# Global scores without repeats, first loads in parts, w_val decoded in pairs, a third buffer for x, a new order

## Chip, core and metric

The kernel runs on one core of one Trainium2 chip. The metric is the time of one execution on the device in microseconds (us). TensorE multiplies matrices, VectorE and ScalarE work on tiles of 128 partitions, and the queues of SyncE (SP) and ScalarE (ACT) start the transfers (DMA). TensorE writes to PSUM, which has eight banks of 512 fp32 columns; all else lies in SBUF.

## What is computed

Attention for 8 batches of 8 heads with 512 local and 32 global positions, head size 64. A global query sees all keys, a local one the global keys and the local keys at most 32 away. The result, as a sequence of 544 positions of 512 values, goes through a causal convolution of 5 taps that makes a gate, and two 512 x 512 matrices:

```python
s_g = scale * np.matmul(q_g, k_all.transpose(0, 1, 3, 2))   # k_all: 32 global keys, then 512 local
out_g = np.matmul(sm(s_g), v_all)
mask = np.abs(pos[:, None] - pos[None, :]) <= 32
s_l = np.concatenate([scale * q_l @ k_g.T, np.where(mask, scale * q_l @ k_l.T, -1e9)], axis=-1)
out_l = np.matmul(sm(s_l), v_all)
x = concatenate([out_g, out_l])        # to (8, 544, 512)
gate = sigmoid(sum(conv_w[k] * xp[:, k:k + S, :] for k in range(5)))
return (gate * (x @ w_val)) @ w_out
```

All inputs and outputs are fp32, but the three arrays of weights lie in memory as 64-bit floats.

## The kernel before

**Units.** Two heads of a batch make one of 32 units; four units make a batch. `qk` is a unit's load: 48 blocks of 32 columns, 16 of local queries, one of global queries, 31 of keys (`KEYS`, L36), in which the block of global keys stands in several places, so that the five blocks that a window of queries needs can be read with one stride (`window`, L59).

**Local attention.** `l_s` (L428) makes the scores of a unit: 32 matmul calls of a 64 x 32 tile each, eight side by side on TensorE. What lies outside the window has to be masked. Where the order names `ngN` for a unit (`ON_PE`, L187; units 0 to 15), TensorE adds the mask by 8 matmuls of 512 columns with the bf16 constants `far` and 4 small ones (L434, L440); VectorE then makes the maximum with two plain reductions over PSUM (`l_max`, L465) and a scaling (`l_neg`, L474), and ScalarE's exponential reads PSUM (L482). In the other units VectorE adds the mask, makes the maximum and writes to SBUF, in eight instructions of 128 columns (L469), and the exponential reads SBUF. Then come the reciprocal, the normalization (`l_norm`, on ScalarE or VectorE), a transpose on VectorE (`l_turn`, L507) and for two units together the product with the values (`l_av`, L513: ten groups, "slots", of eight tiles).

**Global attention.** Once a batch `g_s` (L354) makes the scores of its 32 global queries for all heads: 640 columns for each half of the heads, of which 544 are keys and 96 are repeats that the layout of the values weighs with zero. `g_max` (L370) copies the scores to SBUF and takes the maximum, `g_exp` (L376) makes the exponential from SBUF, `g_t` and `g_tc` transpose and copy (five 128 x 128 blocks for each half, one buffer `pgt`), `g_av` (L395) multiplies with the values, once for each half.

**The rest.** The result of a unit is copied to `xc` (two buffers), split into `xh` and `xl`, and run through the taps: on TensorE for units 0 to 3 (`pc`, with diagonal matrices `dg`), else four steps on VectorE (L567). A sigmoid, the first matrix (`g1`, L606, three matmuls for each product), the gate (`gv`), a split (`gh`, `gl`) and the second matrix (`g2`, L643) follow, then the copy out (`ob`) and the store (`st`). The global rows of all batches go through the same at the very end.

**Weights.** `weight(k)` (L290) loads and decodes the 64-bit floats of `w_val` (0 to 3, a block of columns each) and `w_out` (4 to 7) in eight steps `wK.s0` to `wK.s7` on VectorE (`s0` may be on ScalarE) and one, `wK.high`, on either; a step covers 128 x 512.

**Order.** All tasks stand in one list written out by hand, `ORDER` (L75); every engine takes its own in that order. `:ACT` or `:DVE` names the engine, `@` the PSUM banks. `zN` are N matmuls of zeros. The loads come first, in the order `FIRST` (L180, "q0 q1 w0 q2 q3 w1 v0 w2 w3 v1 m0") on SP's queue; the conv weights and `far` are on ScalarE's (L754, L756). Later loads (`iq`, `ig`, `iv`, `wi`) wait for the matmul ahead of them in the list.

Of the kernel before, what the change touches and what calls it, by code (L numbers as in the profile page):

```python
# [32 lines left out]
GQ = NC  # L33
K0 = GQ + 1
PAIRED = (3, 6, 9, 12, 15)
KEYS = [x for c in range(NC) for x in ((c, -1) if c % 3 == 2 else (c,))] + [x for c in PAIRED for x in (c, -1)]  # L36
NB = K0 + len(KEYS)
AT = {c: K0 + c + c // 3 for c in range(NC)}
WITH_G = {c: K0 + NC + NC // 3 + 2 * n for n, c in enumerate(PAIRED)}

# [3 lines left out]
GC = (R + 1) * R * C  # L44
GB = (R + 1) * R - 1
assert KEYS[AT[NC - 1] - K0:][:R + 1][-1] == -1

# [28 lines left out]
cw dg0:DVE dg1:DVE w0.s0:DVE w0.s1 z6.0@0 s0@64 mx0.0 mx0.1 ng0 dg2:ACT dg3:ACT w0.s2 s1@01 z6.1@2 s2@23 exp0.0 exp0.1  # L76
mx1.0 w0.s3 mx1.1 w0.s4 ng1 exp1.0 w0.s5 w1.s0:DVE w0.s6 w1.s1 den0 w0.s7 mx2.0 rec0 exp1.1 ig2 norm0.0:ACT w1.s2 den1
wi4 w0.high:DVE rec1 norm1.0:ACT norm1.1:ACT norm0.1:DVE gs0@46 mx2.1 w3.s0:ACT gmax0.0 ng2 t0 t1 z20.2@0 av0@40 w3.s1
w1.s3 iq4 exp2.0 exp2.1 gexp0.0 xc0:ACT gmax0.1 w1.s4 w3.s2 den2 w1.high:ACT iq5 w1.s5 rec2 norm2.1:ACT w1.s6 halo0
w1.s7 w3.s3 w4.s0:DVE ig3 ig0 gt0.0@2 w4.s1 pc0.0@6 xh0:ACT xl0 xc1:ACT w4.s2 ig1 s3@45 mx3.0 mx3.1 halo1 w4.s3 ng3  # L80
w4.s4 w3.s4 w4.s5 w3.s5 gtc0.0 pc0.1 pc0.2 pc0.3 pc0.4 norm2.0:ACT w3.high:ACT t2 pc1.0@2 xh1:ACT s4@01 exp3.0 exp3.1
conv0.3:ACT w4.s6 w4.high:ACT den3 mx4.0 rec3 mx4.1 iq6 w4.s7 wi5 w3.s6 ng4 pc1.1 norm3.0:DVE gav0.0@5 gexp0.1 gt0.1@6
w3.s7 norm3.1:ACT t3 pc1.2 s5@43 mx5.0 mx5.1 gtc0.1 iq7 exp4.0 w2.s0:ACT w2.s1 exp4.1 ng5 gav0.1 w5.s0:ACT gden0 pc1.3
w2.s2 grec0 exp5.0 exp5.1 pc1.4 xl1 av1@60 xc2:ACT gnorm0 w5.s1 gx0@4 gxc0:ACT conv1.3:ACT w2.s3 den4 w5.s2 w2.s4 rec4
g1.0.1.0@5 w5.s3 xc3:ACT w2.s5 w5.high:ACT xh2:DVE norm4.0:ACT den5 gs1@63 iq8 halo2:DVE w5.s4 ig4 rec5 xl2 iq9
gmax1.0 w5.s5 s6@21 pc2.0@6 mx6.0 g1.0.1.1 xh3:DVE iv2 mx6.1 w5.s6 ng6 w2.s6 gexp1.0 w5.s7 norm4.1:ACT halo3:DVE s7@70
mx7.0 mx7.1 w2.high:DVE norm5.0:ACT ng7 t4 norm5.1:ACT t5 exp6.0 exp6.1 den6 exp7.0 pc2.1 pc2.2 pc2.3 xl3 fix1 wi6
pc2.4 pc3.0@2 pc3.1 rec6 gmax1.1 norm6.1:DVE pc3.2 fix0 exp7.1 pc3.3 den7 w2.s7 pc3.4 ig5 av2@03 norm6.0:ACT rec7
conv3.3:ACT ig6 conv2.3:ACT t6 w6.s0:ACT sig0 gt1.0@6 w6.s1 wi7 g1.0.0.0@2 g1.0.0.1 xc5:ACT norm7.1:DVE s8@34 ig7 sig1
w6.s2 norm7.0:DVE w6.s3 t7 xc4:ACT s9@10 g1.0.0.2 w6.s4 mx8.0 mx8.1 iq10 g1.0.0.3 sig2 mx9.0 w7.s0:DVE w6.s5 gv.0.0  # L90
g1.0.1.2 g1.0.1.3 iq11 gtc1.0 gav1.0@7 ng8 w7.s1 g1.0.2.0@2 w6.s6 sig3 gv.0.1 w6.high:ACT gexp1.1 gt1.1@5 w6.s7 w7.s2
mx9.1 w7.s3 g1.0.2.1 xh4:ACT gh.0.0:ACT gl.0.0 ng9 exp8.0 g1.0.2.2 exp8.1 den8 iv3 gtc1.1 xl4 exp9.0 w7.s4 gh.0.1:ACT
g1.0.2.3 gv.0.2 exp9.1 gav1.1 gden1 s10@56 rec8 ig9 grec1 gs2@13 w7.s5 iq12 gnorm1 gx1@7 tap4:ACT mx10.0 mx10.1
norm8.0:ACT w7.s6 xh5:ACT den9 gmax2.0 ig10 iq13 gxc1:ACT gl.0.1 w7.high:ACT ig11 ng10 tap5:DVE gexp2.0 halo4:ACT
g1.0.3.0@0 g1.0.3.1 g1.0.3.2 gmax2.1 g1.0.3.3 s11@72 gh.0.2:ACT iv4 gv.0.3 halo5:ACT w7.s7 rec9 conv4.0 gl.0.2 xl5 ig8
# [10 lines left out]
g1.1.3.1 g1.1.1.3 xl8 exp13.0 exp13.1 ng15 g1.1.3.2 g1.1.3.3 gv.1.1 exp15.0 exp15.1 av5@51 conv9.1 ig15 iv7 conv8.0
gh.1.1:ACT conv9.2 g1.1.2.2 g1.1.2.3 conv8.1 conv9.3 conv8.2 xc10:ACT den13 conv8.3 gs3@46 gh.1.0:ACT xc11:ACT iq16
iq17 rec13 norm13.1:ACT iq18 gl.1.0 g2.1.2.0@1 g2.1.1.0@2 gl.1.1 iq19 gv.1.2 den15 xh10:ACT gv.1.3 rec15 gmax3.0
st.0.3:ACT halo10:ACT g2.1.0.0@3 g2.1.2.1 gh.1.2:DVE g2.1.1.1 gh.1.3:DVE gl.1.2 halo11:ACT tap11:ACT norm13.0:ACT
gexp3.0 g2.1.0.1 gl.1.3 g2.1.0.2 gmax3.1 tap10:ACT rec14 t13 gt3.0@4 gtc3.0 xh11:DVE norm14.0:ACT norm14.1:DVE t14  # L110
# [73 lines left out]
NG = 2  # L184
# [8 lines left out]
def attention_moe(ctx, tc, qk, vw, vgw, maskd, fard, w_val, convT, w_out, out):  # L193
# [96 lines left out]
    def weight(k):  # L290
# [30 lines left out]
        for n in range(8):  # L321
            tasks[f"w{k}.s{n}"] = lambda n=n: step(n)
# [517 lines left out]
```

## Time and profile before

| | us |
|---|---|
| median of 3 runs | 353.23 |
| lowest and highest | 350.35, 353.97 |
| the profiled execution | 350.34 |
| its span, first to last instruction | 348.5 |

The profile is of one execution. PE is TensorE's matmuls, PEld its weight loads (which overlap matmuls), DVE VectorE, ACT ScalarE. A matmul's end in the trace is modelled, and neighbouring instructions of one engine overlap in it, so the time from one start to the next says what one really costs. PEclk is the granted share of TensorE's clock.

### The profile page before, as it was taken

To read this page: it belongs to the slowest core of one execution; us is meant where nothing else is said; L and a number is where in the kernel's file an instruction comes from. 1 tells how busy PE (TensorE), PEld (TensorE's weight loads), DVE (VectorE), ACT (ScalarE), POOL (GpSimd) and SP (SyncE) were. 2 spreads that over 40 slices of the span, in tenths; PEclk is the share of its full clock that TensorE was granted. 3 is DMA by queue.
4 is the path that set the end of the run, shared out by engine and by line. 5 is a ranking of instruction groups with operands and counts; after the bars stand their busy time and mean duration, and the time that the engine had idled before them with its cause. 6 is when DMAs were issued, how large, how long until landed. Compare 5 with 4: busy or idle time off the path is not lost.

```text
span 348.5 us, 15657 instructions
## 1 busy us (share of the span) xinstructions
PE 334.3 (96%) x6712; PEld 257.7 (74%) x6712; DVE 318.0 (91%) x863; ACT 282.8 (81%) x930; POOL 1.0 (0%) x8
## 2 busy tenths in 40 slices
PE   7879999999999999999999999999999999999995
PEld 4565665867877777787887878777877888788784
DVE  4899999989999899999999999999999997986961
ACT  3799999998998987998999999999887768144140
POOL 1000000000000000000000000000000000000000
PEclk9999999999999999999999999999999999999998
DMA  8958756679467195752823956536530332001032
GB/s 291 382 216 297 244 163 211 214 233 350 138 226 218 26 392 172 235 192 89 293 91 86 396 206 184 184 103 199 171 137 2 115 112 89 4 30 60 32 120 60
DMA packets 19748, 60.67 MB, mean 174 GB/s; under 512 B 2272, under 2 KB 4704, under 8 KB 19680
## 3 DMA queue, kind: packets, MB, share of 16 engines
q1 hardware_dynamic: 17664, 56.47, 47.4%
q10 hardware_dynamic: 2016, 3.22, 2.6%
q8 instruction: 52, 0.85, 1.0%
q14 instruction: 16, 0.13, 0.1%
HBM read 50.76 MB, written 8.91 MB: 171 GB/s over the span
## 4 chain that ended last, share of the span: by engine, by line
PE 78%; DMA 7%; DVE 6%; ACT 5%; issue 1%; SPq 1%; DVEq 0%; ACTq 0%
PE psum L606 25%; PE psum L643 22%; PE psum L521 10%; PE psum L448 7%; PE psum L584 5%; DMA qk<-in_qk_dram 4%; DMA wraw<-in_w_val_dram 3%; PE psum L401 3%; PE psum L385 3%; PE psum L366 3%; ACT pm L482 2%; ACT pm L498 1%; DVE gateg L681 1%; SPq L283 1%; DVE mx L465 1%
## 5 line engine op out<-in xcount | busy, mean ns | idle before, releaser
L567 DVE SCALAR_TENSOR_TENSOR gate<-xc,cw,gate 128x512 f32<-128x512 f32 x112 | 81.2, 745 | 1.0
L606 PE MATMUL psum<-xh,wvh 128*128 128x512 f32 x128 | 53.2, 416 | 0.5 <-ACT pm L482 0.5
L606 PE MATMUL psum<-xl,wvh 128*128 128x512 f32 x128 | 50.9, 398 | 1.1 <-issue 1.0
L643 PE MATMUL psum<-woh,gh 128*128 128x512 f32 x128 | 51.6, 403 | 0.0
L498 ACT ACTIVATE pm<-pm,mx 128x128 f32<-128x128 f32 x156 | 49.8, 416 | 1.8 <-DVE mx L492 1.8
L482 ACT ACTIVATE pm<-pm,mx 128x128 f32<-128x128 f32 x128 | 49.7, 394 | 1.6 <-DVE mx L469 1.5
L643 PE MATMUL psum<-woh,gl 128*128 128x512 f32 x128 | 50.2, 392 | 0.8 <-DVE gl L620 0.8
L606 PE MATMUL psum<-xh,wvl 128*128 128x512 f32 x128 | 50.4, 394 | 0.0
L643 PE MATMUL psum<-wol,gh 128*128 128x512 f32 x128 | 50.0, 391 | 0.0
L482 ACT ACTIVATE pm<-psum,mx 128x128 f32<-128x128 f32 x128 | 45.1, 405 | 1.4 <-DVE mx L474 1.3
L521 PEld LDWEIGHTS psum<-pts,v 32*64 32x64 f32 x2560 | 35.8, 130 | 9.7 <-DVE pts L507 2.3
L521 PE MATMUL psum<-pts,v 32*64 32x96 f32 (+3 forms) x2560 | 39.5, 258 | 2.0 <-DVE pts L507 1.9
L448 PE MATMUL psum<-qk 64*32 64x128 f32 x2048 | 37.6, 272 | 2.7 <-issue 1.5
L507 DVE STREAM_TRANSPOSE pts<-pm 128x1024 f32<-128x1024 f32 x32 | 39.0, 1229 | 0.6 <-ACT pm L498 0.3
L448 PEld LDWEIGHTS psum<-qk 64*32 64x32 f32 x2048 | 31.6, 105 | 7.6 <-issue 3.8
L482 ACT ACTIVATION_READ_ACCUMULATOR pm<-psum,mx 128x1 f32 x128 | 31.5, 246 | 0.0
L606 PEld LDWEIGHTS psum<-xh,wvh 128*128 128x128 f32 x128 | 24.5, 191 | 7.1 <-issue 1.2
L643 PEld LDWEIGHTS psum<-woh,gl 128*128 128x128 f32 x128 | 24.0, 188 | 6.6 <-DVE gl L620 1.2
L469 DVE CUSTOM_DVE_ANT_0 pm<-psum,mask 128x128 f32<-128x128 f32 x128 | 28.4, 284 | 0.4 <-PE psum L448 0.3
L606 PEld LDWEIGHTS psum<-xh,wvl 128*128 128x128 f32 x128 | 24.0, 188 | 6.0 <-issue 0.6
L606 PEld LDWEIGHTS psum<-xl,wvh 128*128 128x128 f32 x128 | 24.1, 188 | 5.8 <-issue 1.7
L643 PEld LDWEIGHTS psum<-woh,gh 128*128 128x128 f32 x128 | 24.1, 188 | 5.6 <-issue 0.7
(122 smaller groups left out, 591.3 us busy)
## 6 DMA issues: line engine op xcount, KB each, us to landing
qk<-in_qk_dram SPq DMA_DIRECT2D x32, 768.0 KB, 6.1
vg<-in_vgw_dram SPq DMA_DIRECT2D x32, 325.0 KB, 4.2
v<-in_vw_dram SPq DMA_DIRECT2D x16, 640.0 KB, 4.9
out_dram<-ob SPq DMA_DIRECT2D x21, 256.0 KB, 3.4
out_dram<-ob ACTq DMA_DIRECT2D x11, 256.0 KB, 3.0
wraw<-in_w_val_dram SPq DMA_DIRECT2D x4, 512.0 KB, 12.1
wraw<-in_w_out_dram SPq DMA_DIRECT2D x4, 512.0 KB, 4.8
out_dram<-obg ACTq DMA_DIRECT2D x1, 256.0 KB, 3.1
```

Of the source, the lines that this page charges most:

```text
L366: on_pe(T.matmul(s[h][SG * c:SG * c + SG, cols], qkt[rows, C * GQ:C * GQ + C], keys, start=True, stop=True))
L385: on_pe(T.transpose(pt[:, a, :], pg[:, at:at + P], ident))
L448: on_pe(T.matmul(s[h][C * j:C * j + C, i, :], qkt[rows, C * m:C * m + C], blocks(qkt[rows], b, (C * ahead, 2), (C * near, 2), (1, C)), sta ...
L469: V.tensor_tensor_reduce(out=pm[:, h, i, :], in0=s[:, i, :], in1=mask[:, (c0 + i > 0) + (c0 + i == HB - 1), :], op0=ALU.add, op1=ALU.min, ...
L482: A.activation(out=pm[:, h, i, :], in_=st[u]["s"][h][:, i, :] if ON_PE[u] else pm[:, h, i, :], func=AF.Exp, bias=mx[:, c:c + 1], scale=SCA ...
L498: A.activation(out=p[:, i, :], in_=p[:, i, :], func=AF.Copy, scale=rec[:, i:i + 1])
L507: V.transpose(out=st[w, "pts"][:, :, R * k:R * k + R].rearrange("p h i a q -> p h (i a q)"), in_=st[u]["pm"].rearrange("p h i c -> p h (i ...
L521: on_pe(T.matmul(x[j // 2][D * h:D * h + D, j % 2, C * first:C * (first + count)], vt[rows, slot, h, :], p, start=(slot == 0), stop=stop))
L567: V.scalar_tensor_tensor(out=acc, in0=xc[:, k:k + SL], scalar=cw[:, u % NDT, k:k + 1], in1=acc, op0=ALU.mult, op1=ALU.add)
L584: on_pe(T.matmul(bank(f"pc{u}.0"), diag[(u * KW + k) // NDT][:, (u * KW + k) % NDT, :], st[u]["xc"][:, k:k + SL], start=(k == 0), stop=(k ...
L606: on_pe(T.matmul(bank(f"g1.{key}.{e}.0")[:, :n], w[:, e, t * P:t * P + P], x, start=(t == 0 and q == 0), stop=(t == NDT - 1 and q == 2)))
L643: on_pe(T.matmul(bank(f"g2.{key}.{r}.0"), g, w, start=(e == 0 and q == 0), stop=(e == NDT - 1 and q == 2)))
```

## The change

- **Global scores.** The layout of `qk` is new: the eight blocks of local queries of units' first halves stand first, the eight of the second halves and the global queries last, and the keys between. The second matmul of a pair in `g_s` reads the last local block and the global block, 64 columns in place of 160: 544 columns, no repeats. `g_max` is a plain reduction over PSUM, a new `g_neg` scales the two maxima of a batch, and `g_exp` reads PSUM and writes both halves side by side. `g_t` makes four and five transposes, as one block of global keys serves both halves; `g_av` takes both halves in one visit.
- **First loads.** Units 0 and 1 are loaded in two parts, the first 30 blocks ahead of the other 18, unit 0 on ScalarE's queue, unit 1 on SP's; the conv weights move to SP's queue, and `far` comes between the parts.
- **w_val.** Blocks 0 and 1, and 2 and 3, are decoded together, in steps of 128 x 1024.
- **`l_av`.** The groups of eight tiles are put together by width.
- **`xc`** has three buffers. The steps of the convolution of the global rows are no longer interleaved for two blocks.
- **Order.** A new list. `ng5` to `ng15` are gone, so units 5 to 15 are masked on VectorE. The first scores stand ahead of the decoding of the conv weights, the zeros are z6, z21 and z13 where they were z6, z6 and z20 (four fp32r zeros more ahead of the list), and some 110 tasks change engine, among them ten casts `gh` from ScalarE to VectorE on balance, three normalizations and three taps from VectorE to ScalarE on balance, and two copies `xc` to ScalarE.

```diff
-GQ = NC
-K0 = GQ + 1
-PAIRED = (3, 6, 9, 12, 15)
...
+QUERIES = ([*range(0, 4), *range(8, 12)], [*range(4, 8), *range(12, 16)])
+PAIRED = ((3, 9, 12), (6, 15))
+RUN = [x for c in range(NC) for x in ((c, -1) if c % 3 == 2 else (c,))]
+KEYS = [[x for c in p for x in (c, -1)] for p in PAIRED]
+KEYS = KEYS[0] + RUN + KEYS[1]
...
+HEAD = AT[12]
...
-GC = (R + 1) * R * C
...
+GC = (NC + 1) * C
...
+s0@02 s1@13 cw dg0:DVE dg1:DVE dg2:ACT z6.0@4 s2@45 mx0.0 mx0.1 ng0 exp0.0 exp0.1 dg3:DVE mx1.0 mx1.1 ng1 exp1.0 den0
+exp1.1 rec0 w0.s0:ACT norm0.0:DVE gs0@06 norm0.1:DVE t0 den1 mx2.0 rec1 norm1.1:ACT gmax0.0 gmax0.1 norm1.0:ACT mx2.1
+gng0 gexp0.0 w0.s1 ng2 exp2.0 exp2.1 w0.s2 t1 z21.1@2 av0@02 w0.s3 w0.s4 w0.s5 w0.s6 wi4 den2 iq4 iq5 w0.high:ACT
...
+XC = 3
...
-    def transfer(out, in_):
+    def transfer(out, in_, queue=nc.sync):
...
+                box["a"] = sb.tile([P, n, DM], I32, tag="pts" if of_val else "ob", name=f"wa{k}", bufs=2)
...
+    def load_qk(u, queue=nc.sync, cols=slice(0, NB * C)):
+        if cols.start == 0:
+            loads.setdefault(u, [None, None])[0] = sb.tile([P, NB * C], F32, tag="qk", name=f"qk{u}", bufs=4)
+        transfer(loads[u][0][:, cols], qk[u, :, cols], queue)
...
-                    keys, cols = blocks(qkt[rows], AT[15], (1, GC - 15 * C)), slice(15 * C, GC)
...
+                    keys, width = blocks(qkt[rows], AT[15] - 1 if h else WITH_G[15], (1, 2 * C)), 2 * C
...
-        V.tensor_tensor_reduce(out=raw, in0=gst[b]["s"][h], in1=zero.to_broadcast([P, GC]), op0=ALU.add, op1=ALU.min,
-                               scale=-SCALE, scalar=3.0e38, accum_out=gm)
+        if h == 0:
+            gst[b]["gm"] = sb.tile([P, 2], F32, tag="gm", name=f"gm{b}")
+        V.tensor_reduce(out=gst[b]["gm"][:, h:h + 1], in_=gst[b]["s"][h], axis=mybir.AxisListType.X, op=ALU.max)
+
+    def g_neg(b):
+        gm = gst[b]["gm"]
+        V.tensor_scalar(out=gm, in0=gm, scalar1=-SCALE, scalar2=None, op0=ALU.mult)
...
+        A.activation(out=pg[:, GC * h:GC * h + GC], in_=gst[b]["s"][h], func=AF.Exp, bias=gst[b]["gm"][:, h:h + 1],
+                     scale=SCALE)
...
-                at = slot - j % 2
+                at = turn if turn <= HB else 0 if j % 2 else HB + 1
...
+        xc = st[u]["xc"] = sb.tile([P, KW - 1 + SL], F32, tag="xc", name=f"xc{u}", bufs=XC)
...
-        A.dma_start(craw, convT.bitcast(I32))
+        nc.sync.dma_start(craw, convT.bitcast(I32))
+        parts = slice(0, C * HEAD), slice(C * HEAD, C * NB)
+        load_qk(0, A, parts[0])
+        load_qk(1, cols=parts[0])
         if any(ON_PE):
             A.dma_start(far, fard)
-        for x in FIRST.split():
+        load_qk(0, A, parts[1])
+        load_qk(1, cols=parts[1])
+        for x in FIRST.split()[2:]:
...
+        zeros(4, 7)
```

## Rows read from the trace of the kernel before

**Rows 1.** The page, part 1: busy time, share of the span, instructions

```profile
PE 334.3 (96%) x6712; PEld 257.7 (74%) x6712; DVE 318.0 (91%) x863; ACT 282.8 (81%) x930; POOL 1.0 (0%) x8
```

**Rows 2.** Busy time of the engines in four stretches

```profile
core 0: us, PE busy (x) PEld busy (x) DVE busy (x) ACT busy (x) POOL busy (x), PEclk, DMA share, GB/s
0.00:26.00 26.00, 19.80 (x458) 14.28 (x459) 20.10 (x59) 18.18 (x75) 0.96 (x8) 1.00 0.82 298
...
100.00:140.00 40.00, 39.17 (x925) 29.92 (x924) 37.73 (x106) 35.73 (x124) 0.00 (x0) 1.00 0.57 195
...
180.00:260.00 80.00, 79.66 (x1773) 62.98 (x1773) 77.94 (x264) 76.45 (x242) 0.00 (x0) 1.00 0.54 182
...
300.00:340.00 40.00, 39.20 (x194) 32.78 (x193) 32.30 (x70) 12.71 (x26) 0.00 (x0) 1.00 0.14 53
```

**Rows 3.** Timeline of the start: start us, us, engine, line, what; idle before

```profile
7.52 0.41 PE L434 MATMUL psum<-far 64*32 64x512 bf16 x8 [1.58 <-DMA far<-in_far_dram]
...
15.45 0.43 DVE L237 TENSOR_SCALAR wa<-wraw 128x512 int32<-128x512 int32 x1 [1.06 <-DMA wraw<-in_w_val_dram]
...
16.29 4.85 PE L689 MATMUL psum<-zr 128*128 128x512 f32 x20
...
23.05 2.44 PE L521 MATMUL psum<-pts,v 32*64 32x256 f32 x160 [1.91 <-DVE pts L507]
```

**Rows 4.** TensorE: timeline rows, then groups by shape (busy us, mean ns)

```profile
38.09 0.41 PE L434 MATMUL psum<-far 64*32 64x512 bf16 x8
...
39.40 0.78 PE L401 MATMUL psum<-vg,pgt 128*32 128x65 f32 x40
...
161.16 2.03 PE L448 MATMUL psum<-qk 64*32 64x128 f32 x128
163.12 0.78 PE L401 MATMUL psum<-vg,pgt 128*32 128x65 f32 x40
...
268.44 0.71 PE L385 MATMUL psum<-ident,pg 128*128 128x128 f32 x5
...
L366 PE MATMUL psum<-qk 64*32 64x480 f32 x128 | 8.6, 571 | 0.0
L366 PE MATMUL psum<-qk 64*32 64x160 f32 x128 | 4.6, 296 | 0.0
...
L521 PE MATMUL psum<-pts,v 32*64 32x96 f32 x1536 | 27.9, 253 | 0.0
L521 PE MATMUL psum<-pts,v 32*64 32x64 f32 x512 | 20.5, 227 | 0.0
```

**Rows 5.** VectorE: two timeline rows eight reductions apart, then groups by shape

```profile
162.74 0.27 DVE L469 CUSTOM_DVE_ANT_0 pm<-psum,mask 128x128 f32<-128x128 f32 x1
...
164.42 0.69 DVE L620 TENSOR_TENSOR gl<-gv,gh 128x512 fp32r<-128x512 f32 x1
...
L465 DVE TENSOR_REDUCE mx<-psum 128x4 f32<-128x512 f32 x32 | 20.9, 680 | 1.6 <-PE psum L448 1.5
...
L373 DVE CUSTOM_DVE_ANT_0 pgr<-psum,zero 128x640 f32<-128x640 f32 x16 | 12.9, 809 | 0.2 <-PE psum L366 0.2
...
L500 DVE TENSOR_TENSOR pm<-pm,mx 128x512 f32<-128x512 f32 x25 | 16.8, 678 | 0.1
...
L273 DVE CAST gh<-gv 128x512 fp32r<-128x512 f32 x9 | 3.7, 416 | 0.1
```

**Rows 6.** ScalarE: timeline rows, then groups by shape (idle before, releasers)

```profile
22.11 0.34 ACT L482 ACTIVATE pm<-psum,mx 128x128 f32<-128x128 f32 x1
...
22.45 0.35 ACT L482 ACTIVATE pm<-psum,mx 128x128 f32<-128x128 f32 x1
...
163.75 0.40 ACT L482 ACTIVATE pm<-pm,mx 128x128 f32<-128x128 f32 x1
...
164.15 0.39 ACT L482 ACTIVATE pm<-pm,mx 128x128 f32<-128x128 f32 x1
...
L377 ACT ACTIVATE pg<-pgr,gm 128x640 f32<-128x640 f32 x16 | 13.4, 838 | 0.5 <-ACT ob L271 0.4
...
L271 ACT COPY xc<-psum 128x512 f32<-128x512 f32 x30 | 17.6, 599 | 8.7 <-DVE gate L567 7.1 <-PE psum L521 1.6
```

More of the change, by code (lines that the diff above doesn't have):

```diff
@@ L81 @@
[L81 to L95, printed above, removed]
@@ L106 @@
[L106 to L110, printed above, removed]
@@ L278, in on_pe @@
         last_pe[:] = [ins.ins]
-    def transfer(out, in_):
-        ins = nc.sync.dma_start(out, in_).ins
+    def transfer(out, in_, queue=nc.sync):
+        ins = queue.dma_start(out, in_).ins
         if last_pe:
@@ L355, in g_s @@
         units = [loads[u][0] for u in range(NDT * b, NDT * b + NDT)]
-        s = [banks(f"gs{b}", 2, h).rearrange("p a c -> p (a c)")[:, C:C + GC] for h in range(2)]
+        s = [banks(f"gs{b}", 2, h).rearrange("p a c -> p (a c)") for h in range(2)]
+        o = [(C, SL), (SL, SL - 2 * C)]
         for part in range(2):
@@ L362, in g_s @@
                 if part == 0:
-                    keys, cols = blocks(qkt[rows], AT[0], (4 * C, 5), (1, 3 * C)), slice(0, 15 * C)
+                    keys, width = blocks(qkt[rows], AT[0], (4 * C, 5), (1, 3 * C)), 15 * C
                 else:
-                    keys, cols = blocks(qkt[rows], AT[15], (1, GC - 15 * C)), slice(15 * C, GC)
-                on_pe(T.matmul(s[h][SG * c:SG * c + SG, cols], qkt[rows, C * GQ:C * GQ + C], keys,
-                               start=True, stop=True))
@@ new lines, in g_s @@
+                on_pe(T.matmul(s[h][SG * c:SG * c + SG, o[h][part]:o[h][part] + width], qkt[rows, C * GQ:C * GQ + C],
+                               keys, start=True, stop=True))
+        gst[b] = {"s": [s[h][:, min(o[h]):min(o[h]) + GC] for h in range(2)],
+                  "xg": sb.tile([P, 2, D], F32, tag="xg", name=f"xg{b}")}
+    def g_max(b, h):
+        if h == 0:
+            gst[b]["gm"] = sb.tile([P, 2], F32, tag="gm", name=f"gm{b}")
+        V.tensor_reduce(out=gst[b]["gm"][:, h:h + 1], in_=gst[b]["s"][h], axis=mybir.AxisListType.X, op=ALU.max)
@@ L389, in g_tc @@
-        pgt = gst[b]["pgt", h] = sb.tile([P, R + 1, P], F32, tag="pgt", name=f"pgt{b}_{h}", bufs=1)
-        A.copy(pgt, pt[:, :R + 1, :])
+        n = R + h
+        if h == 0:
+            gst[b]["pgt"] = sb.tile([P, len(SLOTS), P], F32, tag="pgt", name=f"pgt{b}", bufs=1)
+        A.copy(gst[b]["pgt"][:, R * h:R * h + n, :], gst[b]["pt", h][:, :n, :])
     def global_av(b):
-        return bank(f"gav{b}.0")[:, :2 * E1].rearrange("p (h d) -> p h d", h=2)
-    def g_av(b, h):
-        pgt = gst[b]["pgt", h]
-        ag = global_av(b)[:, h, :]
-        for a in range(R + 1):
-            for c in range(NDT):
-                vt = loads[NDT * b + c][1]
-                on_pe(T.matmul(ag[SG * c:SG * c + SG, :], pgt[:, a, SG * c:SG * c + SG],
-                               vt[:, a, h, :], start=(a == 0), stop=(a == R)))
+        return bank(f"gav{b}")[:, :2 * E1].rearrange("p (h d) -> p h d", h=2)
@@ L404, in g_den, with g_av @@
+    def g_av(b):
+        pgt = gst[b]["pgt"]
+        for h in range(2):
+            ag = global_av(b)[:, h, :]
+            for a in range(R + 1):
+                for c in range(NDT):
+                    vt = loads[NDT * b + c][1]
+                    on_pe(T.matmul(ag[SG * c:SG * c + SG, :], pgt[:, R * h + a if a < R else 2 * R, SG * c:SG * c + SG],
+                                   vt[:, a, h, :], start=(a == 0), stop=(a == R)))
     def g_den(b):
@@ L699, in attention_moe, with conv_g @@
     gp = []
-    paired = set()
-    def conv_pair(n):
-        if n not in paired:
-            paired.add(n)
-            for k in range(KW):
-                for dt in (2 * n, 2 * n + 1):
-                    gp[dt][2](k)
+    def conv_g(dt):
+        for k in range(KW):
+            gp[dt][2](k)
     def store_g(r, o, c=1):
@@ L786, in _layout @@
     vgw = np.ones((NU, R, C, GS, 2, E1), v_l.dtype)
-    vgw[:, :, :, :R, :, :D] = vl.reshape(NU, R, R, C, 2, D).transpose(0, 1, 3, 2, 4, 5)
-    vgw[:, 0, :, R, :, :D] = vg
-    vgw[:, 1:, :, R] = 0.0
+    vgw[:, :, :, R] = 0.0
+    for h in range(2):
+        vgw[:, :, :, :R, h, :D] = vl[:, GKEYS[h]][:, :, :, h].reshape(NU, R, R, C, D).transpose(0, 2, 3, 1, 4)
+        vgw[:, h, :, R, h, :D] = vg[:, :, h]
+        vgw[:, h, :, R, h, D] = 1.0
     vgw = vgw.reshape(NU, P, GS, 2, E1)
```

260 lines of the change are left out of this document (134 added, 126 removed).

## The prediction

> **What bounds the kernel now.** The page's busy shares come first: TensorE 96%, VectorE 91%, ScalarE 81% [rows 1]. A matmul's end is modelled, so 96% doesn't mean that TensorE works at its peak; the table of busy time by stretches says more [rows 2]. Four stages differ. From 0 to 26 us VectorE is busy for 20.1 us and TensorE for 19.8, and part of TensorE's work there is matmuls of zeros, which only fill. From 100 to 140 us all three engines are nearly full: 39.2, 37.7 and 35.7 of 40. From 180 to 260 they are fuller still: 79.7, 77.9 and 76.5 of 80. From 300 to 340 ScalarE is nearly done (12.7 of 40), VectorE has 7.7 us to spare, and TensorE is full. [...]
>
> So the kernel is bound by waits in its first 26 us, by three engines together up to about 260 us, and by TensorE alone after that. Work taken from TensorE counts in full in the last stage, and only in part in the middle, where VectorE is next in line.
>
> The start, by the timeline [rows 3]: the first scores begin at 7.52 us, after 1.58 us of waiting for the small load of the mask constants behind the first key loads. VectorE then waits 1.06 us at 14.4 for the second block of w_val. Twenty matmuls of zeros run from 16.29 for 4.85 us (0.24 each), and the first product with values starts at 23.05, 1.91 us after the zeros, held up by VectorE's transposes. The start is one chain (load, scores, maximum, exponential, normalize, transpose), and what shortens it is worth its full length as long as the stages behind it keep up.
>
> **The change, part by part: TensorE.** (1) The new order has no `ng5` to `ng15`, so eleven units get their mask on VectorE and not by TensorE's `far` matmuls. A unit with them takes 38.09 to 39.40 = 1.31 us; two without take 161.16 to 163.12, 0.98 each [rows 4]. Eleven times 0.33 is 3.6 us less. (2) Global scores: the second matmul of each pair has 64 columns and not 160. The rows give 571 ns for 480 columns and 296 for 160, so 0.86 ns a column; eight tiles run side by side, each in two passes, so 96 x 0.86 x 2 = 0.165 us a batch, 1.3 us in all. (3) Nine transposes a batch in place of ten: between nothing and a fifth of the 0.71 us that five take; I take 0.1, so 0.8 us. (4) The products with values: one group of eight shrinks from 96 columns at its widest to 64, one from 64 to 32. The rows of 96 and 64 columns are 26 ns apart; I count the second the same at most, so up to 0.1 us in each of 16 visits. The bounds are 0 and 1.7 us; I take 1.2, as neighbours run in lockstep in the rows. Together TensorE loses 6.9 us of real work. Zeros go from 32 to 44 matmuls: 12 x 0.24 = 2.9 us more, at the start, where TensorE waits anyway; uncovered they would cost those 2.9 us.
>
> **VectorE.** (1) A masked unit is eight reductions that start 0.21 us apart (162.74 to 164.42 is 1.68 us); a unit masked by TensorE is two reductions of 0.68, which overlap their neighbours by some 0.07 each as the eight do, and a small scaling, by my estimate 0.1, since it covers 8 columns: 1.3 us [rows 5]. So 0.4 x 11 = 4.4 us more. (2) The global maximum: 16 instructions of 809 ns over 640 columns become plain reductions over 544. At the 680 ns for 512 columns that is about 0.72, so 16 x 0.09 = 1.4 us less, and eight scalings of 0.1 come in: 0.6 less net. (3) w_val in pairs: 14 instructions fewer. 680 ns for 512 columns and 809 for 640 make 1.0 ns a column and 0.16 us fixed, of which 0.07 overlap: 14 x 0.09 = 1.3 less. Four more of its steps go to ScalarE and one comes back, at the 0.42 of a cast: 1.3 less. (4) Moves between engines: nine casts `gh` to VectorE at 0.42 (+3.8), three normalizations away at 0.68 (-2.0); five small diagonals come and three taps, two copies of x and some small ones go, each at most 0.68, so between -4 and +1, of which I take -2.0. Sum: 4.4 - 0.6 - 2.6 + 3.8 - 2.0 - 2.0 = +1.0 us, so VectorE stays as full as it was. Some 4 us of it move into 45 to 115 us, where the eleven units lie.
>
> [...]
>
> **ScalarE.** Masked units read the exponential from SBUF: starts 0.40 us apart in place of 0.34 [rows 6], 88 instructions, 0.05 x 88 = 4.4 more. The global exponential reads 544 columns from PSUM rather than 640 from SBUF: 838 ns now, and near the 599 of a 512-column copy from PSUM after, so some 0.2 x 16 = 3.2 less. The first copy of global weights shrinks from 640 to 512 columns, 0.1 x 8 = 0.8 less. Moves: ten casts and five diagonals away, w_val steps, normalizations, taps and copies of x in; by the same rows about +1. Net some +1 us, and ScalarE is not the bound after 260. The third buffer for x removes a wait of ScalarE for VectorE that is 7.1 us in all [rows 6], most of it on an engine with slack: worth nothing by itself, at most the 1 to 2 us by which it lets products be copied out earlier.
>
> **The start.** The first 30 of 48 column blocks of units 0 and 1 come ahead of the rest, on two queues. Of 1.5 MB that the first scores need, 0.96 MB are left; at the 298 GB/s of the first stage 0.58 MB are 1.9 us. `far` now stands behind a head on ScalarE's queue, so I take 1.5 for the first scores. VectorE no longer has decoding ahead of the first maximum, and the wait for the second block of w_val (1.06 us) is covered, since both blocks are decoded later. But loads of units 2 and 3 end no earlier (the bytes ahead of them are the same), and the 21 zeros behind the first global scores start no earlier than 16.3 and take 5.1: the first product starts at about 21.4 and not 23.05. The start is worth 0 to 1.9 us; I take 1.5. What is late next is VectorE, full from there on.
>
> **Sum.** Start -1.5. TensorE after 140 us, where it counts in full: five batches of (2) and (3), twelve visits of (4), 5 x 0.265 + 12 x 0.075 = -2.2. TensorE before that: 6.9 - 2.2 = 4.7, of which I count half, because VectorE and ScalarE are within 2 us in 40 of being the bound: -2.4. VectorE's +1.0 counts half as well: +0.5. That is -5.6 us of a span of 348.5: about 343, and with the 1.8 us outside the span 344.7 for the profiled execution, which took 350.34. The median of the runs shown is 353.23, 0.8% above it; there the same gain gives 347.6. I forecast **347** for the median.
>
> **Rivals.** *VectorE bounds (no change).* If the middle runs at VectorE's pace, TensorE's 4.7 us there are worth nothing, VectorE's +4 us in 45 to 115 us eat the start, and only part of the end's 2.2 us is left: 350 to 353. For it: 77.9 of 80 busy. Against it: the end is TensorE's alone. Chance 0.22.
>
> *All of it counts.* TensorE's 6.9 and 1.9 of the start, and a few waits on late key loads or x buffers gone: 9 to 11 us, so about 343. Against it: VectorE has no room for it. Chance 0.13.
>
> *Slower: PSUM held longer.* Before, the four banks of a batch's global scores were free after the maximum, whose result went to SBUF. Now the exponential reads PSUM, so the banks wait for both maxima, the new scaling and an exponential behind ScalarE's queue. If TensorE stands at the next use of such a bank for two exponentials (2 x 0.7) in each of eight batches, that is 11 us against 5.6 of gain: 358 to 359. It decides from 0.7 us a batch. Against it: the bank numbers in the new order mostly put other banks in between. Chance 0.09.
>
> *The first loads don't do what they should:* the small `far` load, behind 480 KB on its queue, lands as late as before. Then the start is worth 0, and the time 348.5 to 349. Chance 0.06.
>
> The forecast itself has 0.50, with a range of its own of 344 to 350.
>
> **How the numbers follow.** About 1% (3.5 us) is what a measurement of this kernel can tell from no change; the three runs shown spread by 1%. Of the forecast (0.50) some 0.40 lies more than 3.5 us below; with 0.13 where all counts and 0.04 of the loads' rival that is 0.57 faster. Slower by over 1% is the PSUM rival and a little of VectorE's: 0.12. The rest, 0.31, is the same. The range for 8 in 10 leaves out most of the PSUM rival above and the far end of the second rival below: 341 to 354.
>
> **What would show it.** Right: first scores near 6 us, the first product near 21.4; 40 `far` matmuls and not 128; score visits of 0.98 us between 45 and 115; from 140 us TensorE as full as before, with the same tasks some 2 us shorter. Wrong: VectorE at 40 of 40 and TensorE with gaps in 60 to 140 (VectorE bounds); TensorE waiting for ScalarE's exponential at a bank of global scores (PSUM); a first-score time still at 7.5; a granted clock under 1.00 before 340 us, since the zeros have moved.

## The result, and the profile after

The changed kernel takes 347.16 us (median of 4 executions, 345.58 to 347.91), the kernel before, run beside it, 351.97 (350.35 to 353.97). The ratio is 0.9854, with a 95% interval of 0.9812 to 0.9896: 4.8 us or 1.5% faster, against a forecast of 347 and a gain of 5.6. The profiled execution went from 350.34 to 345.58 us, its span from 348.5 to 343.8. Here and below medians are of all executions, while ratios leave out those more than 1.5% above the fastest of their kernel.

The page after, part 1 (busy time, share of the span, instructions):

```profile
PE 329.8 (96%) x6584; PEld 256.1 (74%) x6584; DVE 320.7 (93%) x986; ACT 285.0 (83%) x933; POOL 0.9 (0%) x7
```

Beside [rows 1] TensorE has 4.5 us less, VectorE 2.7 and ScalarE 2.2 more. The busy time in stretches, with the same columns as [rows 2], and two stretches more:

```profile
0.00:26.00 26.00, 21.78 (x541) 15.87 (x542) 21.60 (x56) 19.56 (x73) 0.85 (x7) 1.00 0.81 286
26.00:60.00 34.00, 33.48 (x720) 20.02 (x724) 33.38 (x108) 34.00 (x129) 0.00 (x0) 1.00 0.76 270
60.00:100.00 40.00, 37.70 (x806) 29.55 (x801) 39.08 (x147) 39.02 (x134) 0.00 (x0) 1.00 0.64 210
100.00:140.00 40.00, 39.95 (x928) 31.94 (x917) 39.19 (x128) 39.52 (x128) 0.00 (x0) 1.00 0.59 195
...
180.00:260.00 80.00, 78.73 (x1663) 62.55 (x1662) 77.38 (x250) 74.55 (x230) 0.00 (x0) 1.00 0.56 183
...
300.00:340.00 40.00, 39.11 (x205) 33.09 (x203) 32.75 (x69) 8.27 (x17) 0.00 (x0) 1.00 0.14 53
```

The granted clock is 1.00 in all of them. From 26 to 60 us ScalarE has no free moment. The same stretch of the kernel before, where TensorE runs no zeros:

```profile
26.00:60.00 34.00, 33.92 (x753) 19.13 (x756) 33.47 (x87) 33.76 (x133) 0.00 (x0) 1.00 0.66 231
```

The start, by the timeline (compare [rows 3]): the first scores, the scores of unit 2 behind their load, the 21 matmuls of zeros, and the first product with values, now right behind the zeros.

```profile
6.21 0.41 PE L448 MATMUL psum<-far 64*32 64x512 bf16 x8 [0.80 <-DMA far<-in_far_dram]
...
13.74 1.07 PE L462 MATMUL psum<-qk 64*32 64x128 f32 x57 [2.41 <-DMA qk<-in_qk_dram]
...
15.71 5.06 PE L704 MATMUL psum<-zr 128*128 128x512 f32 x21
20.69 2.41 PE L535 MATMUL psum<-pts,v 32*64 32x256 f32 x160
```

Groups by shape (busy us, mean ns, idle before), as in [rows 4 to 6]: masks, zeros, global scores, products with values, masked reductions, the global exponential.

```profile
L448 PE MATMUL psum<-far 64*32 64x512 bf16 x40 | 2.4, 384 | 0.8 <-DMA far<-in_far_dram 0.8
L704 PE MATMUL psum<-zr 128*128 128x512 f32 x44 | 12.3, 428 | 0.0
L374 PE MATMUL psum<-qk 64*32 64x480 f32 x128 | 8.4, 572 | 0.5 <-ACT xc L277 0.5
L374 PE MATMUL psum<-qk 64*32 64x64 f32 x128 | 2.7, 216 | 0.0
L535 PE MATMUL psum<-pts,v 32*64 32x96 f32 x1536 | 24.0, 253 | 0.0
L535 PE MATMUL psum<-pts,v 32*64 32x64 f32 x512 | 12.8, 222 | 0.0
L483 DVE CUSTOM_DVE_ANT_0 pm<-psum,mask 128x128 f32<-128x128 f32 x216 | 48.4, 284 | 0.7 <-PE psum L462 0.4
L389 ACT ACTIVATE pg<-psum,gm 128x544 f32<-128x544 f32 x16 | 10.8, 709 | 0.0
```

**Where the time went.** TensorE's account closes almost by itself. Zeros are 9.3 and 3.2 us (rounded and plain float32) of its 334.3 before and 12.3 and 3.2 of 329.8 after. Real work is thus 321.8 before and 314.3 after: 7.5 us less. Zeros are 3.0 more. Its idle time is 348.5 - 334.3 = 14.2 before and 343.8 - 329.8 = 14.0 after. Together -7.5 + 3.0 - 0.2 = -4.7, the change of the span: of the 7.5 us taken from TensorE 4.7 show, and most of the rest stands as zeros, which only fill. The zeros alone, in two stretches, show where (busy us of that line's matmuls and weight loads; 11.69 us before in the first stretch and none in the second):

```profile
core 0: us, PE busy (x) PEld busy (x), PEclk, DMA share, GB/s
0.00:26.00 26.00, 11.35 (x35) 7.42 (x35) 1.00 0.81 286
26.00:60.00 34.00, 3.26 (x13) 2.36 (x13) 1.00 0.76 270
```

So the whole of the increase lies behind the start, between 26 and 60 us, where ScalarE is full. These 13 matmuls end at 37.0 us, and the first stop behind them is a wait for ScalarE, which has not been idle since 26:

```profile
44.20 1.15 PE L374 MATMUL psum<-qk 64*32 64x480 f32 x32 [0.52 <-ACT xc L277]
```

Without the zeros TensorE would have come to that wait earlier, and not past it. That is read from the trace; the kernel without them was not run.

### The profile page after: what moved, and what is told of

The parts are those of the page before. It is cut to its first block, busy times and chain, and to the rows that moved or that the text cites. A ratio compares the mean times of both kernels' runs of the same rounds, so it can differ in the third digit from the quotient of the medians.

```text
span 343.8 us, 15523 instructions
## 1 busy us (share of the span) xinstructions
PE 329.8 (96%) x6584; PEld 256.1 (74%) x6584; DVE 320.7 (93%) x986; ACT 285.0 (83%) x933; POOL 0.9 (0%) x7
## 4 chain that ended last, share of the span: by engine, by line
PE 41%; DVE 25%; ACT 19%; DMA 9%; issue 4%; SPq 0%; ACTq 0%; DVEq 0%
PE psum L621 14%; PE psum L658 12%; ACT pm L496 7%; PE psum L535 6%; DVE gate L581 5%; PE psum L462 3%; ACT pm L512 3%; DVE pm L483 3%; DMA vg<-in_vgw_dram 3%; DMA wraw<-in_w_val_dram 3%; DVE pts L521 3%; DVE gateg L696 2%; DVE gv L629 2%; DMA wraw<-in_w_out_dram 2%; ACT xc L277 2%
## 5 line engine op out<-in xcount | busy, mean ns | idle before, releaser
L496 ACT ACTIVATE pm<-pm,mx 128x128 f32<-128x128 f32 x216 | 83.8, 394 | 1.1 <-DVE mx L483 1.1
L512 ACT ACTIVATE pm<-pm,mx 128x128 f32<-128x128 f32 x168 | 52.9, 396 | 0.1
L658 PE MATMUL psum<-woh,gl 128*128 128x512 f32 x128 | 50.1, 392 | 0.0
L483 DVE CUSTOM_DVE_ANT_0 pm<-psum,mask 128x128 f32<-128x128 f32 x216 | 48.4, 284 | 0.7 <-PE psum L462 0.4
L521 DVE STREAM_TRANSPOSE pts<-pm 128x1024 f32<-128x1024 f32 x32 | 39.7, 1239 | 2.2 <-ACT pm L512 1.8
L496 ACT ACTIVATION_READ_ACCUMULATOR pm<-pm,mx 128x1 f32 x216 | 41.7, 193 | 0.0
L535 PE MATMUL psum<-pts,v 32*64 32x96 f32 (+3 forms) x2560 | 38.5, 259 | 1.3 <-ACT pg L389 0.8
L462 PEld LDWEIGHTS psum<-qk 64*32 64x32 f32 x2048 | 29.6, 105 | 11.5 <-DMA qk<-in_qk_dram 3.4
L277 ACT COPY ob<-psum 128x512 f32<-128x512 f32 x29 | 16.3, 578 | 15.1 <-PE psum L658 15.1
```

Source lines behind the costliest of these rows:

```text
L277: A.copy(out, in_)
L462: on_pe(T.matmul(s[h][C * j:C * j + C, i, :], qkt[rows, C * QAT[m]:C * QAT[m] + C], blocks(qkt[rows], b, (C * ahead, 2), (C * near, 2), (1 ...
L483: V.tensor_tensor_reduce(out=pm[:, h, i, :], in0=s[:, i, :], in1=mask[:, (c0 + i > 0) + (c0 + i == HB - 1), :], op0=ALU.add, op1=ALU.min, ...
L496: A.activation(out=pm[:, h, i, :], in_=st[u]["s"][h][:, i, :] if ON_PE[u] else pm[:, h, i, :], func=AF.Exp, bias=mx[:, c:c + 1], scale=SCA ...
L512: A.activation(out=p[:, i, :], in_=p[:, i, :], func=AF.Copy, scale=rec[:, i:i + 1])
L521: V.transpose(out=st[w, "pts"][:, :, R * k:R * k + R].rearrange("p h i a q -> p h (i a q)"), in_=st[u]["pm"].rearrange("p h i c -> p h (i ...
```

## Experiments

Each was timed beside the kernel before; ratios are to that kernel, as above. The changed kernel stands at 0.9854.

**The start.** The changed kernel with its first loads whole, as before (the edit in short):

```diff
-load_qk(0, A, parts[0]); load_qk(1, cols=parts[0]); far; load_qk(0, A, parts[1]); load_qk(1, cols=parts[1])
+A.dma_start(craw, ...); far; then FIRST from its beginning
```

> The changed kernel with its first loads as before: units 0 and 1 whole on SP's queue, the conv weights and the mask constants first on ScalarE's. Theory START (most of the gain is made in the first 46 us, where the same TensorE work is done 3.9 us earlier, and is kept): first scores at 7.3 to 7.6 us in place of 6.21, the conv weights back at 5.4 in place of 3.73, first product 1 to 2 us later than 20.69, total +1 to +2 us against the changed kernel (ratio to the kernel before 0.988 to 0.992). Theory WORK (the gain is TensorE's saved work, and the start only fills a gap that later waits take back): total within 0.5 us of the changed kernel (0.985).

Measured: 347.89 us, 0.9883 (0.9841 to 0.9924), where the first theory had it, but the interval holds the second's 0.985 too. In its profiled execution (span 347.9) the first scores begin at 8.04 us, and the clock is at half while they run:

```profile
8.00:10.00 2.00, 1.96 (x74) 1.74 (x78) 1.54 (x8) 1.05 (x4) 0.00 (x0) 0.50 1.06 423
10.00:12.00 2.00, 2.00 (x84) 1.89 (x76) 1.41 (x4) 0.00 (x0) 0.00 (x0) 0.50 0.99 402
```

The 0.50 lasts from 7.1 to 13.9 us, and TensorE had stood for 3.2 us ahead of these scores. Is it the later scores that cost, or the clock? The same kernel with the wait filled (its first zeros end at 6.60 us and not at 4.82):

```diff
-zeros(4, 7)
+zeros(2, 7, zf)      # plain float32: as many instructions, longer
```

> loads_whole (the changed kernel with the first loads as before; first scores at 8.04 us instead of 6.21) with the 4 us wait ahead of the first scores covered by slower filling matmuls, as many instructions. If what the loads in parts save is the clock that falls behind that wait, the median comes down to the changed kernel's 347.2 or below, ratio 0.982 to 0.986, with a mean clock of 0.997 or more. If it is the earlier first scores, it stays at 347.9 to 349.0, 0.988 to 0.991.

Measured: 348.05 us, 0.9896 (0.9860 to 0.9933). The profiled execution has a mean clock of 1.000 and a span of 346.4, 2.6 us over the changed kernel's:

```profile
7.85 0.41 PE L448 MATMUL psum<-far 64*32 64x512 bf16 x8 [1.25 <-DMA far<-in_far_dram]
...
22.06 2.20 PE L535 MATMUL psum<-pts,v 32*64 32x256 f32 x140 [0.36 <-issue]
```

First scores 1.6 us later, VectorE's transposes ahead of the first product 1.6 later, first product 1.4 later, and at equal work left TensorE is 1.5 us behind at 48 us; the other 1.2 come at 103 us, by a stop that is explained below. So in the traces the delay alone is 1.5 us, as I had it. The half clock of the execution above adds to it: there TensorE is 3.6 us behind at 48 us. In the times the two can't be told apart: with the wait filled the kernel is 0.9 us behind the changed one by the medians and 1.5 by the ratios, without it 0.7 and 1.0, and neither interval is clear of the changed kernel's.

The clock, from the other side: the second gate convolution of the global part in pairs again, alone, and then with longer zeros in both waits of the start.

```diff
+paired = set()       # gconv: taps of two tiles in turn, as before the change
-zeros(4, 7) ... z6.0
+zeros(1, 7, zf); zeros(2, 7) ... z6.0: zeros(2, bank, zf[:, :WARM]); zeros(2, bank)     # second kernel only
```

(That first edit had been tried alone with this expectation.)

> The changed kernel with the steps of the global rows' convolution interleaved for two blocks again. In the changed kernel these 16 instructions start 0.52 us apart, in the kernel before 0.40, so VectorE gets 1.9 us back between 318 and 331, where its work stands in the chain that ended last. If that chain sets the end: -0.5 to -1.5 us against the changed kernel, and TensorE's gap at 330 (0.68) is gone. If TensorE's work alone sets it: within 0.3 us.

Measured: 346.21 us, 0.9838 (0.9797 to 0.9879). TensorE's wait of 0.67 us at 330 is gone, and at equal work left it makes up 0.9 us between 320 and 340: the first theory, by the trace.

> The changed kernel with the second gate convolution of the global part in pairs again (gconv_paired) and with slower filling matmuls in the two waits of the start (4.8 to 6.2 and 11 to 13.7 us): as many instructions, of float32 instead of its rounded form, so that TensorE has work where it waited for the loads. Several executions show the granted clock at half for some us behind these waits (gconv_paired 15.5 to 18.2 us, loads_whole 8.0 to 12.6 us). If the waits bring the fall, every execution has a mean clock of 0.998 or more and the median is 345.0 to 345.8, ratio 0.979 to 0.982. If not, it stays with gconv_paired at 346.2, 0.984.

Measured: 345.65 us, 0.9839 (0.9801 to 0.9876). Three of six executions have a clock of 1.000 (344.84 to 345.54 us), three 0.992 to 0.995 (345.76 to 346.83), so the first expectation is missed. The second wait was not covered: the first scores of unit 2 stand ahead of it, and TensorE waits 2.56 us for their load as before. Whether these waits bring the clock down stays open; the executions in which it fell are about 1 us longer. Neither kernel's interval is clear of the changed kernel's.

**The masks.** Eleven units moved their masks to VectorE. First the move alone, in the old order, for the six units where it is possible:

```diff
-ng5 ng7 ng12 ng13 ng14 ng15      # taken from the old ORDER
```

> The kernel before with six units (5, 7, 12 to 15) masked on VectorE, nothing else changed: -6 x 0.33 = 2.0 us of TensorE, +2.4 of VectorE, +2.4 of ScalarE. If TensorE binds: -2 us against the kernel before (0.994). If VectorE or ScalarE binds: +2.4 (1.007). Shared: within 0.7 us (0.998 to 1.002).

Measured: 369.46 us, 1.0481 (1.0426 to 1.0536): 17 us slower, which none of the theories allows for. Then the move back in the changed kernel:

```diff
+ng5 ng6 ng7 ng8 ng9 ng12 ng13    # each behind its mxN.1
```

> The changed kernel with seven units (5 to 9, 12, 13) masked by TensorE again: +7 x 0.33 = 2.3 us of TensorE, -7 x 0.4 = 2.8 us of VectorE, and ScalarE's exponential of these units from PSUM (-7 x 0.4 = 2.8). If TensorE binds 45 to 105 us: +2 us. If VectorE binds there: -2 to -2.8 us. If they share the bound, as the prediction counted (half of each): within 0.7 us of the changed kernel.

Measured: 379.55 us, 1.0794. In this kernel some of these units' exponentials read PSUM banks that the new order has already given to other tasks (unit 7's bank 5 goes to unit 8's scores first), so a part of its local attention is computed from other numbers. It prices nothing, and what the masks' move is worth in the new order is not shown by any run.

**Work added.** To see which engine bounds which stage, four doses in the changed kernel:

```diff
+dpN ahead of sN:     14 transposes of ident into a bank       (TensorE)
+dvN behind mxN.1:     7 reductions of ident, 128 columns each (VectorE)
```

> The changed kernel with 14 more 128x128 transposes of the constant identity ahead of the scores of units 8, 9, 10 and 11 (58 to 87 us). By the nine transposes of the changed kernel, which took 1.2 to 1.4 us, one dose is 1.5 to 2.2 us, four are 6 to 8. If the three engines share the bound there, as my halves assumed, about half of it shows at the end: +3 to +4 us over the changed kernel's 347.2, ratio 0.994 to 0.998. If VectorE bounds the middle, +0 to +1: 0.985 to 0.989. If TensorE bounds it, all of it: 1.003 to 1.009.

> The same dose of 56 transposes ahead of the scores of units 23, 24, 26 and 28 (189 to 226 us), where I counted TensorE's savings in full. In full: +6 to +8 us over the changed kernel, ratio 1.003 to 1.009. If there the bound is shared too: +3 to +4, 0.994 to 0.998. If another engine bounds it: 0.985 to 0.989.

> The changed kernel with 7 more 128x128 reductions on VectorE behind the maxima of units 8, 9, 10 and 11: 0.21 us from start to start in the changed kernel, so 1.5 us a dose and 6 us in all. Shared bound: +3 us over the changed kernel, ratio 0.994. VectorE bounds the middle: +6, 1.003. TensorE bounds it: +0 to +1, 0.985 to 0.989.

> The same 28 reductions behind the maxima of units 23, 24, 26 and 28, where I counted TensorE's work in full and VectorE's at nothing. By that +0 to +1 us, ratio 0.985 to 0.989; with a shared bound +3, 0.994; where VectorE bounds it +6, 1.003.

Measured: TensorE's dose early 368.83 us, 1.0472 (1.0428 to 1.0516), late 358.10, 1.0174 (1.0132 to 1.0216); VectorE's early 354.67, 1.0070 (1.0041 to 1.0099), late 355.15, 1.0103 (1.0068 to 1.0139). The doses themselves (TensorE's of the late run, VectorE's of the early one):

```profile
L668 PE MATMUL psum<-ident 128*128 128x128 f32 x56 | 6.8, 273 | 0.0
```

```profile
L668 DVE TENSOR_REDUCE table<-ident 128x1 f32<-128x128 f32 x28 | 8.0, 286 | 0.8
```

TensorE's is as planned. VectorE's is larger: its reductions start 0.32 us apart, not 0.21, so a run's 28 take 8.5 us and not 6. They cost 7.5 early and 8.0 late: about in full in both places, and nowhere at half or at nothing. (In the late run's trace the clock is at half for two stretches of 3.4 us among the doses, so some of its cost may be the clock's.) A dose on VectorE also stands between a unit's maximum and its exponential, so it may cost by the delay of that chain as well as by VectorE's time; the runs don't part the two. TensorE's 6.8 cost 21.7 and 10.9, three times and one and a half times themselves. Its stops show why. In the early run:

```profile
176.43 0.44 PE L437 MATMUL psum<-pts,v 32*64 32x32 f32 x9 [4.55 <-issue]
```

In the middle of a product with values, with 9 of 160 matmuls to go, TensorE stands for 4.55 us and waits for nothing that the profile shows.

**Where TensorE's instructions lie.** I numbered TensorE's records of the trace (matmuls, weight loads, its own waits) in order and looked at the number of the first one behind each stop. In the early run the seven longest stops in products with values fall on 3522, 5057, 6594, 7105, 8386, 11457 and 12738. All of them leave 193 or 194 on division by 256. The page's list of transfers has a queue for instructions, here with its packets, MB and share of the changed kernel:

```profile
q8 instruction: 51, 0.84, 1.0%
```

That is 16 KB a packet for some 13,200 records, 259 to a packet, and so, by the remainders, 256 records of 64 bytes. Each of the seven stops ends 2.3 to 2.8 us after a packet began, and that packet began 0.5 to 3.8 us after TensorE had gone past the limit before it; from one packet to the next it is never less than 3.3 us. Stops at that remainder sum to 2.6 us in the kernel before, 2.1 in the changed one, 13.9 and 6.7 in the runs with TensorE's doses, 1.6 and 2.0 with VectorE's, and 10.7 in masks_alone_on_vector. A product with values is 320 instructions in 2.4 us: where two limits of packets fall into such a run, the second packet is late. A dose on TensorE puts 28 instructions in and so moves every limit behind it. Without the stops beyond the changed kernel's 2.1 the doses cost 9.9 us early (where the clock is 0.93 from 0 to 26 us and 0.94 from 140 to 180) and 6.3 late, where 6.8 are in full. Another reading needs no subtraction: at equal work left, the doses not counted, the late run is 0.9 us behind the changed kernel at 185 us, ahead of its doses, and 6.6 at 260, ahead of its long stops; the early run goes from 1.6 at 57 us to 7.0 at 100. So TensorE's dose counts for 5.4 to 5.7 us of 6.8, nearly in full too. Doses that keep the number of TensorE's instructions were not run. If the place of the limits is the cause, moving them and nothing else must cost as much:

```diff
 z21.1:
-zeros(21, bank)
+zeros(16, bank); small(69, bank)      # 69 bf16 matmuls of 32 columns: 128 instructions more, by my estimate in the same 5 us
```

> In the dosed kernels TensorE stops, 0.4 to 4.6 us at a time, always at the same place in a run of 256 of its instructions, and goes on 2.2 to 2.9 us after a 16 KB packet of instructions began (13.9 us of such stops in tensor_dose_early, 6.7 in tensor_dose_late, 10.7 in masks_alone_on_vector, 2.1 in the changed kernel, 2.6 in the kernel before). Here 21 filling matmuls ahead of the first value product become 16, with 69 small ones (32 columns) behind them: 64 more pairs of load and matmul, so every later instruction stands 128 places further, in about the same 5 us, and nothing else differs. If the place of the code in its packets costs time, it shows here: with the limits moved by 128 in the changed kernel's own trace, 14 pairs of them would follow each other in less than 3.3 us, 19 us short in all at most; as each stop gives slack to the next I expect +8 to +19 us over the changed kernel's 347.2, ratio 1.010 to 1.041. If the doses cost more than their size for another reason (buffers, the order), +0 to +1: 0.985 to 0.989.

Measured: 369.39 us, 1.0478 (1.0425 to 1.0530), 22 us over the changed kernel for the same work, a little above the range that I had for it. The page, part 1:

```profile
PE 334.6 (91%) x6648; PEld 258.7 (71%) x6648; DVE 321.8 (88%) x986; ACT 285.9 (78%) x933; POOL 0.8 (0%) x7
```

The group of the products with values (1.3 us of idle time before them in the changed kernel):

```profile
L535 PE MATMUL psum<-pts,v 32*64 32x96 f32 (+3 forms) x2560 | 41.3, 259 | 16.3 <-issue 15.1 <-DVE gv L629 0.5 <-ACT pg L389 0.4
```

Two rows of the timeline:

```profile
167.79 2.25 PE L535 MATMUL psum<-pts,v 32*64 32x256 f32 x143 [0.27 <-ACT pgt L403]
174.78 0.52 PE L535 MATMUL psum<-pts,v 32*64 32x64 f32 x17 [4.73 <-issue]
```

And the list of transfers from 172.2 to 172.5 us, all packets and those of instructions:

```profile
DMA packets 13, 0.05 MB, mean 178 GB/s; under 512 B 6, under 2 KB 6, under 8 KB 12
...
q8 instruction: 1, 0.02, 18.8%
```

The packet of instructions begins 2.3 us after TensorE has run dry, and 2.4 us later TensorE goes on. From 170.0 to 172.2 the list has 160 packets and none of this queue, and the transfer engines are busy to over 95% there. Ahead of other stops they were idle (two of the early dose's seven), so other transfers may lengthen a stop but aren't needed for one. Stops at the remainder sum to 20.6 us. The mean granted clock is 0.971 to 0.986 in these executions; in the trace it is 0.50 from 173.0 to 179.8 us, from within the stop shown, and from 46.7 to 50.1, behind one of 2.4 us. TensorE's idle time is 32.1 us against 14.0.

With this the masks could be priced. masks_alone_on_vector again, with 12 small matmuls in each of the six units for the 12 that left:

```diff
+elif u in (5, 7, 12, 13, 14, 15):
+    for n in range(12): on_pe(T.matmul(o[:, 0, :C], one[rows], far[rows, P:P + C], start=True, stop=True))
```

> masks_alone_on_vector (the masks of units 5, 7 and 12 to 15 of the kernel before on VectorE) with 12 small matmuls in each of these units in the place of the 12 removed, so that all of TensorE's instructions stand where they stand in the kernel before. What they add is 6 times about 0.2 us. If the place of the code is the larger cause of its +17 us, 8 us of it go (10.7 less 2.6 us of stops): about 361, ratio 1.022 to 1.027. If buffers of the exponentials (ACT waits 5.8 us for the transposition there) are the cause, it stays at 368 to 370, 1.045 to 1.053.

Measured: 356.03 us, 1.0133 (1.0092 to 1.0174). Of the 17 us 13 are gone, more than the 8 that I expected, with the stops down from 10.7 to 1.8 us. What stays is 4.8 us, about 1.2 of it the filling itself by my estimate above. ScalarE's wait for the transpose, which frees one of three buffers `pm` (a masked unit opens its buffer at the maximum and not at the exponential), is there in both, first without the filling and then with it:

```profile
ACT pm L383 <- DVE pts L408: 5.8, 3, 2.3
```

```profile
ACT pm L388 <- DVE pts L413: 5.7, 3, 2.3
```

The kernel before has no such wait among those listed for ScalarE. So the masks' move by itself, for six units in the old order and with TensorE's instructions in place, is a loss. Whether it is a gain in the new order is not shown. The new code in the old order was not run, since it moves every limit of packets as well. Nor were the masks of units 10, 11, 14 and 15 put back, or two buffers for x, which the new order doesn't allow.

## Why the prediction was right, step by step

**The start: right, by the traces.** I took 1.5 us and a first product at 21.4. The first scores came 1.3 us earlier, the first product at 20.69, 2.4 us earlier: the wait of 1.91 us for VectorE's transposes is gone, as I had it, and the zeros began at 15.71 and not at 16.3, which I had not. Undoing the loads with the wait filled puts TensorE 1.5 us behind in the trace; in the times its cost of 0.9 to 1.5 us is not clear of noise. Their rival (`far` as late as before) is out: 6.21 against 7.52.

**TensorE's savings: right in sum, by errors that cancel, which is luck.** 7.5 us are measured, 6.9 were predicted. 40 `far` matmuls instead of 128 are the eleven units, but term (1) is mis-sized. I set one unit with masks, 1.31 us, against two without that stand together, 0.98 each. A single one without masks, ahead of the same task, takes 203.11 - 202.03 = 1.08 us in the kernel before:

```profile
202.03 1.16 PE L448 MATMUL psum<-qk 64*32 64x128 f32 x64
203.11 0.77 PE L401 MATMUL psum<-vg,pgt 128*32 128x65 f32 x40
```

That makes 11 x 0.23 = 2.5 us and not 3.6; counted from start to start without idle time, all local scores with their masks went from 38.7 to 36.4 us. Term (2) held: a visit of global scores takes 1.08 us against 1.24, the 0.165 that I had. Term (3) came to nothing: 72 transposes in place of 80, counted the same way, take 8.5 us against 8.4. Term (4): a visit of products with values went from 2.37 to 2.34 us, 0.03 less where I took 0.075. Against these stands what I left out. Both halves' global values in one visit take 1.28 us where two visits took 0.70 each, 0.12 in each of eight batches, and the first matrix (100.6 to 99.4 us, counted the same way) and the taps on TensorE (17.9 to 17.3) take less for a reason that was not looked for.

**"Half of it counts" failed as a reason.** I let TensorE's savings before 140 us and VectorE's extra work count half, since all engines were nearly full there. From 60 us to the end TensorE had 6.0 us less to do and took 4.8 less (280.5 us of work before and 274.5 after, without zeros and with overlaps counted once; spans of 288.5 and 283.8); 0.8 of the missing 1.2 are stops at packet limits. And a dose cost about its full length on VectorE, and nearly its full length on TensorE, early and late. So work added or taken was passed on nearly in full there. The stage that did eat the gain was one that I had not read, 26 to 60 us. That 4.7 of TensorE's 7.5 us show, about the share of my 4.6 of 6.9, is therefore luck: the share is right, the stage and the reason are not.

**The zeros failed in place.** I put 2.9 us more of zeros into the start, where TensorE waits anyway. They came to 3.0, but the start has no more of them than before; 13 stand between 26 and 60 us, ahead of a wait for ScalarE, which has no free moment there. By 60 us TensorE has done 41.1 us of its work and the kernel before 42.2, although the first product came 2.4 us earlier. Full savings of 7.5 less 3.0 happen to lie near my 5.6; that is luck too.

**VectorE: +1.0 predicted, +2.7 measured.** The large term held: masked reductions start 0.21 us apart and last 284 ns. The single moves that make up the rest of the 1.7 us were not told apart.

**The rivals.** VectorE as the only bound would have left 350 to 353; 347.2 lies below it. The gap that I named as its sign is there (37.70 of 40 from 60 to 100 us), but its longest part, 1.54 us at 80.1, is a stop at a packet limit. PSUM held longer: TensorE's only wait listed for the global exponential is one of 0.8 us, not 0.7 in each of eight batches.

```profile
75.71 2.41 PE L535 MATMUL psum<-pts,v 32*64 32x256 f32 x160 [0.76 <-ACT pg L389]
...
81.64 0.39 PE L621 MATMUL psum<-xh,wvh 128*128 128x512 f32 x1 [1.54 <-issue]
```

"All of it counts" was the nearer rival in its mechanism from 60 us on; its time of 343 had no stage in it that eats the gain.

**What I didn't see:** that an edit of TensorE's program, useful or not, can cost some 5 to 20 us by where it moves the code. Nothing in my range held that. The changed kernel lies well by this measure, as the one before did (2.1 and 2.6 us of stops).

## What to carry over

Where an engine runs hundreds of short instructions in a few microseconds, count its stops by the instruction's number as well as by the tile: stops that share a remainder are the code's, and an experiment there must keep the number of instructions, or it measures the shift. Account for the engine that is full (real work, filling, idle) before and after, and look for the stage in which a gain is filled up again. In an order written out for one set of works, a dose on any engine can show in full, so a discount for "nearly full" engines needs a stage of its own to stand on. And compare like with like when a saving is read from two rows: one visit with one, ahead of the same task.

## What the runs showed of the hardware

- TensorE's instructions come in packets of 16 KB (51 for 13,206 records in the changed kernel, so about 256 to a packet), never less than 3.3 us from one to the next, and a stop of TensorE at a packet's limit ends 2.2 to 3.2 us after the packet's start. These stops sum to 2.1 us in the changed kernel and to 20.6 with its code moved by 128 places (code_shifted).
- At a stand of TensorE of 3.2 us (loads_whole) and of 4.7 us (code_shifted) the granted clock fell to half for 6.8 us, and behind one of 2.4 us for 3.4 (code_shifted, at 46 us). Behind another of 2.5 us (at 243 us) it stayed at 1.00; what decides it was not found.
- The doses' reductions on VectorE (plain, from SBUF, all into one tile; vector_dose_early) start 0.32 us apart, the masked ones of as many columns 0.21; why was not looked for.
